# Fourteen matmuls of the identity by itself ahead of the first scores of a sparse attention and feed-forward kernel

## The chip, the core and the metric

One core of one Trainium2 chip runs the whole kernel. The metric is the device time of one execution in microseconds; of several runs the median stands.

## What is computed

The reference is a block-sparse attention followed by a gated feed-forward layer, all in float32.

```python
scores = scale * np.matmul(q, k.transpose(0, 1, 3, 2))        # q, k, v: 4 x 8 x 768 x 64
mask = np.abs(blk_i - blk_j) <= 1                             # blocks of 32 positions
mask = mask | (blk_i == 0) | (blk_j == 0) | (blk_i == 23) | (blk_j == 23)
...
        mask[qb*32:(qb+1)*32, kb*32:(kb+1)*32] = True         # three sampled blocks a query block
scores = np.where(mask, scores, -1e9)
attn = np.exp(scores - np.max(scores, axis=-1, keepdims=True))
attn = attn / (np.sum(attn, axis=-1, keepdims=True) + 1e-09)
x = np.matmul(attn, v)                                        # then 3072 tokens x 512
h = x @ w_in                                                  # 512 x 2048
g = h * (1.0 / (1.0 + np.exp(-1.702 * h)))
return g @ w_out                                              # 2048 x 512
```

## The kernel before

The attention is cut into units: 64 query positions of one batch entry, with all eight heads. Eight units make a chunk of 512 tokens, and the feed-forward layer takes one chunk at a time, while the units of the next chunk are worked on in between. The first chunk has no feed-forward work to lie beside, and its eight units are run by `first()`, in an order that is written out by hand in the string `ORDER`: each entry is a letter for a step and the number of a unit. S is `scores` (TensorE, L301: 16 matmuls of 64x32 by 256 columns for a unit, into two banks of PSUM), L the minima on VectorE (`least`, L324), E the exponentials on ScalarE (L336), T `transposes` by TensorE against the identity (L352), C the copies of these on ScalarE (L357), V `values` (L376), N the normalisation (L430), R `turn`, two more transposes (L441), H the split of their result into two parts (L448, L449), X and Y copies of keys and values that two units share, W one step of the conversion of the feed-forward weights, and G n the arrival of the n-th key buffer. The string begins "X1 G0 G1 G2 G3 S0 S1 L0 E0 L1 X2 T0 E1 S2 S3", so TensorE's queue begins with the scores of units 0 and 1, the transposes of unit 0 and the scores of units 2 and 3. The instructions keep the order in which the code issues them.

G steps put work on GpSimd's queue: a small copy that waits for the key buffer's DMAs (`landed`, L771), then the gathers of value blocks (indirect DMAs, L253), and for G3 and G4 the first fetches of the weights (L474). G4 also refills key buffer 0 from SP, behind a DMA that waits for the minima of unit 6 (L783). The weights come as 64-bit words and are turned into float32 on ScalarE and VectorE (L486 to L531), each in time for the feed-forward step that needs it.

The identity is a constant tile of 128x128 float32, `self.ident`. GpSimd writes it in `indices()`, ahead of all this, with the helper in masks.py (a memset, then an affine select). Before, its first reader is the first transpose of unit 0. The eight banks of PSUM are `self.bank[0]` to `self.bank[7]`; in the first chunk the scores use banks 0, 1, 4 and 5, the transposes 3 and 7.

The feed-forward layer multiplies in two ways. For the first eight of the 16 slices of the hidden dimension in the first chunk, `down` (L608) is a plain float32 matmul of 128x128 by 128x512. All the rest (L563 to L565, L618 to L623) are matmuls of operands that were split into a high and a low part of type float32r.

Of the kernel before, what the change touches and what calls it, by code (L numbers as in the profile page):

```python
# [18 lines left out]
P = 128  # L19
# [22 lines left out]
AHEAD = 5  # L42
NFULL = 8
FIRST = CU // 2
ORDER = """X1 G0 G1 G2 G3 S0 S1 L0 E0 L1 X2 T0 E1 S2 S3 L2 C0 T1 C1 Y1 V0 N0 L3 X3 V1 E2 T2 R0 N1 E3 H0 S4 R1 S5 C2 T3 L4 H1
V2 N2 E4 C3 L5 Y2 T4 C4 R2 H2 E5 V3 N3 S6 L6 R3 G4 S7 H3 L7 E6 T5 V4 C5 Y3 V5 N4 E7 W W R4 T6 C6 N5 W R5 H4 H5 T7 C7 W
V6 N6 W V7 W R6 W N7 H6 R7 H7 W"""
# [2 lines left out]
class Kernel:  # L50
# [4 lines left out]
    def __init__(self, ctx, tc, q, qd, kb, kT, v, vd, sb, w_in, w_out, out):  # L55
# [29 lines left out]
        self.vmid += spare[4:6]  # L85
        self.kmidof, self.vmidof = [None] * FIRST, [None] * FIRST
        self.units, self.kent, self.vent, self.items = [], [], [], []
# [23 lines left out]
        for of in (self.kent, self.vent):  # L111
            for e in of:
                e["at"] = e["n"] if e["n"] < FIRST else e["n"] % RING
        self.knext = self.vnext = FIRST
        self.most = {"scores": FIRST + 1, "values": FIRST + 1}
        self.early, self.turned = True, False
# [3 lines left out]
    def indices(self):  # L120
# [7 lines left out]
        def take(shape):  # L128
            n = 1
            for k in shape:  # L130
# [8 lines left out]

        vblk = take([NB])  # L140
        first, second = slice(1, NB - 2, 2), slice(2, NB - 1, 2)
        nc.gpsimd.iota(vblk[3 * BLK:P, first], pattern=[[2, NU]], base=0, channel_multiplier=0,
                       allow_small_or_imprecise_dtypes=True)
# [21 lines left out]
        for i in range(NR):  # L165
            for cols, rows in ((first, slice(BLK * i, BLK * (i + 1))), (second, slice(BLK * (i + 1), BLK * (i + 2)))):
                nc.vector.tensor_copy(out=vblk[rows, cols], in_=sbw[rows, cols, i])
# [28 lines left out]
    def load_k(self, e):  # L196
# [9 lines left out]
        nc.sync.dma_start(out=self.qt[r].rearrange("p b c -> p (b c)"), in_=self.q[:, b // 2, u])  # L206
        if 0 < e["n"] < FIRST:
            nc.sync.dma_start(out=kg[:, 1:9:7], in_=kb[:, q0 + 1:q0 + 3])
# [6 lines left out]
        self.sampled(e, 0, nc.sync)  # L215
        if e["n"] >= FIRST or e["n"] == 0:
            self.sampled(e, 1, nc.sync if e["n"] else nc.scalar)
# [237 lines left out]
    def weights(self):  # L455
# [40 lines left out]
        for k in range(3, AHEAD):  # L496
            fetch(k)
        yield
        first(0)
        yield  # L500
        for k, (f, i) in enumerate(todo):
# [261 lines left out]
    def first(self):  # L763

        nc, items = self.nc, self.items[:CU]
        assert self.items[CU]["unit"]["n"] == CU
        work = {}

        def landed(r):

            nc.gpsimd.tensor_copy(out=self.seen[:, 0:NPAIR].rearrange("p (a b) -> p a b", a=2), in_=self.kg[r][:, 6:12:5, 0, 0:2])  # L771

        def ahead(n):

            if n < FIRST:
                landed(n)
                self.gather(self.vent[n])
                if n + 2 < FIRST:
                    self.sampled(self.kent[n + 2], 1, nc.gpsimd)
                if n == FIRST - 1:  # L780
                    next(self.conv)
            else:
                nc.sync.dma_start(out=self.seen[:, NPAIR:2 * NPAIR], in_=items[2 * n - 2]["unit"]["nm"][:, 0])  # L783
                self.load_k(self.kent[self.knext])
                self.knext += 1
                landed(0)
                next(self.conv)
                self.loads()

        for step in ORDER.split():  # L790
            what, n = step[0], int(step[1:] or 0)
            g = items[n]
            if what == "G":
                ahead(n)
            elif what == "W":
                next(self.conv)
            elif what == "X":
                for to, of in ((0, 8), (7, 1)):
                    nc.vector.tensor_copy(out=self.kg[n][:, to], in_=self.kg[n - 1][:, of])
            elif what == "Y":  # L800
                nc.vector.tensor_copy(out=self.vmid[n][UT:P], in_=self.vmid[0][UT:P])
            elif what == "S":
                work["L", n], *work["E", n] = self.scores(g)
                work["L", n] = [work["L", n]]
            elif what == "T":
                work["C", n] = self.transposes(g)
                self.turned = n == CU - 1
            elif what == "V":
                work["N", n] = self.values(g)
            elif what == "R":  # L810
                work["H", n] = self.turn(g)
            else:
                for f in work.pop((what, n)):
                    f()
        assert not work
        x1 = self.const.tile([P, 2, NCT, CT], F32R, name="x1")
        self.x.append((x1[:, 0], x1[:, 1]))
        wout = self.const.tile([P, WRING, 2 * DM], F32R, name="wout")
        self.wout = [wout[:, i] for i in range(WRING)]
# [66 lines left out]
```

## Time and profile before

| | us |
|---|---|
| three runs: median (lowest to highest) | 772.25 (770.96 to 776.37) |
| the profiled execution: its own time | 773.84 |
| its span, from the first to the last instruction | 771.2 |
| TensorE busy in the span | 740.8 |
| VectorE, ScalarE, GpSimd busy | 408.1, 375.8, 69.8 |

The span is 2.6 us shorter than the execution's own time, since the profile begins with the first instruction of the program. All times in rows are counted from there. PE is TensorE's matmul, PEld its weight load, DVE VectorE, ACT ScalarE, POOL GpSimd, SP SyncE, which issues DMAs; a name with a q behind it (SPq) is the instruction queue of that engine. A matmul of plain float32 leaves more than one record; "x64" counts records.

### The profile page before, as it was taken

To read this page: it belongs to the slowest core of one execution; us is meant where nothing else is said; L and a number is where in the kernel's file an instruction comes from. 1 tells how busy PE (TensorE), PEld (TensorE's weight loads), DVE (VectorE), ACT (ScalarE), POOL (GpSimd) and SP (SyncE) were. 2 spreads that over 40 slices of the span, in tenths; PEclk is the share of its full clock that TensorE was granted. 3 is DMA by queue.
4 is the path that set the end of the run, shared out by engine and by line. 5 is a ranking of instruction groups with operands and counts; after the bars stand their busy time and mean duration, and the time that the engine had idled before them with its cause. 6 is when DMAs were issued, how large, how long until landed. Compare 5 with 4: busy or idle time off the path is not lost.

```text
span 771.2 us, 18922 instructions
## 1 busy us (share of the span) xinstructions
PE 740.8 (96%) x7424; PEld 563.5 (73%) x7424; DVE 408.1 (53%) x1069; ACT 375.8 (49%) x938; POOL 69.8 (9%) x112
## 2 busy tenths in 40 slices
PE   2879999999999999999999999999999999999997
PEld 1555666777787777778778777778777777888885
DVE  3588988885544434554454454454555344433332
ACT  2675666765554453544444444444554454333232
POOL 4324212120000000000000000000000000000000
PEclk9999999999999999999999999999999999999999
DMA  8979996675742546554444454345564321141211
GB/s 227 299 257 388 370 347 223 205 235 177 241 159 74 184 139 207 149 166 154 123 141 148 146 166 156 124 130 159 179 210 145 101 81 42 29 109 42 55 41 55
DMA packets 64251, 126.88 MB, mean 165 GB/s; under 512 B 7617, under 2 KB 30402, under 8 KB 63650
## 3 DMA queue, kind: packets, MB, share of 16 engines
q1 hardware_dynamic: 51970, 83.78, 36.1%
q0 software_dynamic: 11376, 41.03, 15.5%
q8 instruction: 58, 0.95, 0.5%
q10 hardware_dynamic: 816, 0.86, 0.4%
q14 instruction: 31, 0.25, 0.1%
HBM read 115.16 MB, written 10.49 MB: 163 GB/s over the span
## 4 chain that ended last, share of the span: by engine, by line
PE 92%; DMA 2%; DVE 2%; issue 1%; ACT 1%; another core or an unknown queue 1%; SPq 1%; ACTq 0%; DVEq 0%
PE bank L563 12%; PE bank L564 11%; PE bank L565 11%; PE bank L622 11%; PE bank L623 10%; PE bank L618 10%; PE bank L352 6%; PE bank L376 6%; PE bank L301 6%; PE bank L608 3%; PE bank L396 2%; PE bank L313 2%; PE bank L441 1%; DMA win<-in_moe_w_in_dram 1%
## 5 line engine op out<-in xcount | busy, mean ns | idle before, releaser
L578 DVE SCALAR_TENSOR_TENSOR g<-g,bank 128x512 f32<-128x512 f32 x83 | 57.1, 688 | 185.6 <-ACT g L571 185.6
L336 ACT ACTIVATE ex<-bank,nm 128x256 f32<-128x256 f32 (+1 forms) x176 | 84.6, 490 | 119.8 <-DVE nm L324 119.8
L622 PE MATMUL bank<-wout,ghi 128*128 128x512 f32 x352 | 141.6, 402 | 0.0
L623 PE MATMUL bank<-wout,ghi 128*128 128x512 f32 x352 | 139.5, 396 | 0.0
L571 ACT ACTIVATE g<-bank 128x512 f32<-128x512 f32 x96 | 57.3, 597 | 154.9 <-PE bank L565 153.0
L618 PE MATMUL bank<-wout,glo 128*128 128x512 f32 x352 | 99.1, 395 | 0.0
L552 DVE TENSOR_TENSOR wout<-wst,wout 128x512 fp32r<-128x512 f32 x80 | 55.4, 693 | 79.6 <-ACT wout L551 78.7
L324 DVE CUSTOM_DVE_ANT_1 bank<-bank,bias 128x256 f32<-128x256 f32 x176 | 73.8, 440 | 20.1 <-remote 8.6
L563 PE MATMUL bank<-xhi,win 128*128 128x512 f32 x192 | 80.6, 420 | 0.5 <-ACT xhi L448 0.5
L563 PE MATMUL bank<-x,win 128*128 128x512 f32 x192 | 78.8, 410 | 0.2 <-DVE g L578 0.2
L585 ACT CAST ghi<-g 128x512 fp32r<-128x512 f32 x88 | 54.7, 621 | 49.8 <-DVE g L578 49.7
L618 PEld LDWEIGHTS bank<-wout,glo 128*128 128x128 f32 x352 | 66.1, 188 | 16.0
L622 PEld LDWEIGHTS bank<-wout,ghi 128*128 128x128 f32 x352 | 66.2, 188 | 15.3
L623 PEld LDWEIGHTS bank<-wout,ghi 128*128 128x128 f32 x352 | 66.3, 188 | 14.7
L564 PE MATMUL bank<-x,win 128*128 128x512 f32 x192 | 76.1, 396 | 0.0
L564 PE MATMUL bank<-xlo,win 128*128 128x512 f32 x192 | 75.9, 395 | 0.0
L565 PE MATMUL bank<-xhi,win 128*128 128x512 f32 x192 | 75.6, 394 | 0.0
L565 PE MATMUL bank<-x,win 128*128 128x512 f32 x192 | 75.4, 393 | 0.0
L253 POOL DMA_INDIRECT vown<-in_v_dram,vidx x40 | 39.4, 986 | 380.7 <-PE bank L376 268.4
L357 ACT COPY pt<-bank 128x512 f32<-128x512 f32 (+1 forms) x112 | 56.8, 563 | 20.9 <-PE bank L352 20.9
L593 DVE TENSOR_TENSOR glo<-g,ghi 128x512 fp32r<-128x512 f32 x88 | 60.3, 685 | 1.4 <-ACT ghi L585 1.4
L301 PE MATMUL bank<-kg,qt 64*32 64x256 f32 x1280 | 47.0, 393 | 14.0 <-DMA qt<-in_q_dram 13.4
(135 smaller groups left out, 1047.3 us busy)
## 6 DMA issues: line engine op xcount, KB each, us to landing
wst<-ws SPq DMA_DIRECT2D x80, 256.0 KB
kg<-in_kb_dram SPq DMA_DIRECT2D x114, 128.0 KB
kg<-in_kb_dram SPq DMA_DIRECT2D x42, 256.0 KB
win<-in_moe_w_in_dram POOLq DMA_DIRECT2D x16, 512.0 KB
raw<-in_moe_w_out_dram POOLq DMA_DIRECT2D x16, 512.0 KB
kg<-in_kT_dram SPq DMA_DIRECT2D x4, 1536.0 KB
vown<-in_vd_dram SPq DMA_DIRECT2D x8, 768.0 KB
out_dram<-raw SPq DMA_DIRECT2D x41, 128.0 KB
```

The lines of the kernel that those rows point to most:

```text
L301: nc.tensor.matmul(sps[h][BLK * c:BLK * (c + 1), n * i:n * (i + 1)].rearrange("p (g n s) -> p g n s", g=2, s=BLK), self.qt[r][rows, bi, UT ...
L324: nc.vector.tensor_tensor_reduce(out=at, in0=at, in1=bias, scale=-SCALE, scalar=3.0e38, op0=ALU.add, op1=ALU.min, accum_out=un["nm"][:, ha ...
L336: nc.scalar.activation(out=ex, in_=sps[h][:, n * k:n * (k + 1)], func=AF.Exp, bias=un["nm"][:, half, c:c + 1], scale=-1.0, accum_out=un["r ...
L563: nc.tensor.matmul(h, wih[:, k], hi[:, k], start=(k == 0), stop=False)
L564: nc.tensor.matmul(h, wih[:, k], lo[:, k], start=False, stop=False)
L565: nc.tensor.matmul(h, wil[:, k], hi[:, k], start=False, stop=(k == NCT - 1))
L571: nc.scalar.activation(out=g, in_=self.h, func=AF.Tanh, scale=0.851)
L578: nc.vector.scalar_tensor_tensor(out=g, in0=g, scalar=1.0, in1=h, op0=ALU.add, op1=ALU.mult)
L593: self.nc.vector.tensor_tensor(out=glo, in0=g, in1=ghi.bitcast(F32), op=ALU.subtract)
L618: nc.tensor.matmul(o[n], glo[:, tk[n]], woh, start=False, stop=last)
L622: nc.tensor.matmul(o[n], ghi[:, tk[n]], woh, start=(f == 0), stop=False)
L623: nc.tensor.matmul(o[n], ghi[:, tk[n]], wol, start=False, stop=False)
```

## The change

Fourteen matmuls are issued on TensorE ahead of the loop over `ORDER`. Stationary and moving operand are the identity, the moving one read four times over, so that each has 512 columns; the result goes into bank 7, each time anew, and nobody reads it.

```diff
+WARM = 14
...
+        many = self.ident.rearrange("p (o c) -> p o c", o=1).broadcast_to([P, 4, P])
+        for _ in range(WARM):
+            nc.tensor.matmul(self.bank[7].rearrange("p (o c) -> p o c", o=4), self.ident, many, start=True, stop=True)
         for step in ORDER.split():
```

TensorE's queue at the head of the program, before: a branch into the program, then the scores of unit 0 (bank_85 and bank_86 are banks 0 and 1, kg_93 and qt_95 the first keys and queries), the first of which wait for DMAs.

```order
0 L882 UNCONDITIONAL_BRANCH [waits barrier_Pool_Activation_PE_DVE_SP_release]
1 L301 MATMUL bank_85<-kg_93,qt_95 32x256 [waits DMAHW4_49,DMAHW3_49,DMAHW6_49,DMAHW2_49,DMAHW0_49]
2 L301 MATMUL bank_86<-kg_93,qt_95 32x256
3 L301 MATMUL bank_85<-kg_93,qt_95 32x256 [waits DMAHW7_49,DMAHW5_49,DMAHW1_49]
4 L301 MATMUL bank_86<-kg_93,qt_95 32x256
```

The same place now (bank_92 is bank 7; the line numbers behind the edit are larger, L302 is what was L301).

```order
0 L886 UNCONDITIONAL_BRANCH [waits barrier_Pool_Activation_PE_DVE_SP_release]
1 L793 MATMUL bank_92<-ident 128x512 [waits Pool_49]
2 L793 MATMUL bank_92<-ident 128x512 x13
3 L302 MATMUL bank_85<-kg_93,qt_95 32x256 [waits DMAHW4_49,DMAHW3_49,DMAHW6_49,DMAHW2_49,DMAHW0_49]
4 L302 MATMUL bank_86<-kg_93,qt_95 32x256
5 L302 MATMUL bank_85<-kg_93,qt_95 32x256 [waits DMAHW7_49,DMAHW5_49,DMAHW1_49]
6 L302 MATMUL bank_86<-kg_93,qt_95 32x256
```

The scores stand behind fourteen matmuls that wait for GpSimd once, and keep their own waits for DMAs.

Further on in TensorE's queue, the transposes of unit 0 before (bank_88 and bank_92 are banks 3 and 7, ghi and glo the exponentials):

```order
33 L352 MATMUL bank_88<-ident,ghi 128x128 [waits Activation_49,Pool_49]
34 L352 MATMUL bank_88<-ident,ghi 128x128
35 L352 MATMUL bank_88<-ident,ghi 128x128 [waits Activation_49]
36 L352 MATMUL bank_88<-ident,ghi 128x128
37 L352 MATMUL bank_92<-ident,glo 128x128 [waits Activation_49]
```

And now:

```order
35 L353 MATMUL bank_88<-ident,ghi 128x128 [waits Activation_49]
36 L353 MATMUL bank_88<-ident,ghi 128x128
37 L353 MATMUL bank_88<-ident,ghi 128x128 [waits Activation_49]
38 L353 MATMUL bank_88<-ident,ghi 128x128
39 L353 MATMUL bank_92<-ident,glo 128x128 [waits Activation_49]
```

The wait for GpSimd, which wrote the identity, went from the first transpose to the first of the new matmuls; the transposes into bank 7 have no new wait. The other engines' instructions stand as they stood.

## Rows read from the trace of the kernel before

**Rows 1.** The page: busy time, and three lines of the 40 slices.
```profile
PE 740.8 (96%) x7424; PEld 563.5 (73%) x7424; DVE 408.1 (53%) x1069; ACT 375.8 (49%) x938; POOL 69.8 (9%) x112
...
PE   2879999999999999999999999999999999999997
...
PEclk9999999999999999999999999999999999999999
```
**Rows 2.** The chain of waits, 0 to 110 us: start, length, what.
```profile
10.90 6.12 another core or an unknown queue
17.02 0.41 DVE bank L324
...
18.83 0.81 PE bank L352 x4
...
26.42 1.11 issue
...
47.21 1.40 issue
...
59.08 7.03 DMA win<-in_moe_w_in_dram
...
67.82 1.20 PE bank L301 x32
...
72.02 3.43 PE bank L608 x8
```
**Rows 3.** Timeline of GpSimd: start, length, what, idle time before and releaser.
```profile
3.48 0.29 POOL masks.py:199 TENSOR_SCALAR_AFFINE_SELECT ident<-ident 128x128 f32<-128x128 f32 x1
...
54.99 0.53 POOL L771 COPY seen<-kg 128x4 f32<-128x4 f32 x1 [13.82 <-DMA kg<-in_kb_dram]
```
**Rows 4.** Timelines of TensorE's matmuls and weight loads, 13 to 30 us.
```profile
13.40 4.45 PE L301 MATMUL bank<-kg,qt 64*32 64x256 f32 x64 [13.40 <-DMA qt<-in_q_dram]
...
20.48 2.76 PE L301 MATMUL bank<-kg,qt 64*32 64x256 f32 x64
...
28.92 0.38 PE L441 MATMUL bank<-ident,x 128*128 128x128 f32 x2
...
16.87 0.33 PEld L301 LDWEIGHTS bank<-kg,qt 64*32 64x32 f32 x14 [0.55 <-issue]
...
29.23 0.70 PEld L301 LDWEIGHTS bank<-x 64*32 64x32 f32 x32 [0.17 <-DMA x<-in_kb_dram]
```
**Rows 5.** Instructions by line: 13.4 to 17.0, 17.45 to 17.5, 20.6 to 23 us; busy, mean ns.
```profile
L301 PE MATMUL bank<-kg,qt 64*32 64x256 f32 x56 | 4.2, 629 | 13.4 <-DMA qt<-in_q_dram 13.4
...
L301 PE MATMUL bank<-kg,qt 64*32 64x256 f32 x14 | 1.0, 523 | 0.0
...
L301 PE MATMUL bank<-kg,qt 64*32 64x256 f32 x64 | 2.8, 381 | 0.0
```
**Rows 6.** L608 alone: least, median and longest ns of one record.
```profile
L608 PEld LDWEIGHTS bank<-ghi,g x32: 186/190/192, 63.6 to 116.5; 128*128 128x128 f32 x32
L608 PE MATMUL bank<-ghi,g x32: 591/592/697, 63.6 to 117.0; 128*128 128x512 f32 x32
```
**Rows 7.** Windows: length, PE, PEld, DVE, ACT, POOL busy; clock, DMA share, GB/s.
```profile
44.00:52.00 8.00, 6.12 (x122) 4.82 (x120) 5.30 (x19) 6.64 (x23) 0.00 (x0) 1.00 0.92 316
52.00:54.00 2.00, 1.83 (x67) 1.60 (x67) 1.77 (x7) 1.51 (x4) 0.00 (x0) 1.00 0.30 86
...
80.00:760.00 680.00, 677.52 (x6553) 521.08 (x6546) 352.93 (x886) 328.50 (x809) 40.48 (x50) 1.00 0.48 150
```
**Rows 8.** VectorE's timeline at 17 us; SP's waits: in total, times, longest.
```profile
17.01 0.43 DVE L324 CUSTOM_DVE_ANT_1 bank<-bank,bias 128x256 f32<-128x256 f32 x1 [6.11 <-remote]
...
SPq L783 <- DVE xlo L449: 13.3, 1, 13.3
```
**Rows 9.** Window of L301 alone, TensorE: length, busy, clock, DMA share, GB/s.
```profile
13.40:15.50 2.10, 2.10 (x40) 1.00 1.07 289
```

## The prediction

> **What bounds the kernel now.** I read the page's shares first, then the chain that ended last, then the timelines of single engines around the place of the edit. TensorE is busy for 740.8 of 771.2 us, and the slices show where it is not: the first and second slice of 19.3 us each, and the end [rows 1]. From 80 to 760 us it is busy for 677.5 of 680 us, in the windows [rows 7]; nothing in front of the program can be won back or lost there, so whatever happens to the first units either reaches 68 us as a shift of everything, or is swallowed before. The question is therefore one of the first 68 us alone.
>
> In those the chain runs as follows [rows 2]: DMAs, from 10.90 on a stretch of 6.12 us that it puts down to an unknown queue, the first `least` on VectorE at 17.02 (L324), the exponentials, the first transposes on TensorE at 18.83 (L352), and then mostly TensorE, with three pieces called issue (the first of 1.11, the last of 1.40 us), in which it waits for nothing that the profile shows. At 59.08 a load of w_in takes the chain for 7.03 us, and from 67.82 on TensorE never lets go. The timeline puts names to the first stretch: the first scores start at 13.40, released by a DMA, and with the second unit's take 4.45 us for 64 records; the same 64 records at 20.48 take 2.76 us [rows 4].
>
> Why 4.45? The page's clock row shows full speed in every slice [rows 1], but one scores matmul of the first pair takes 629 ns, at 17.5 us 523 on average, and later 381 [rows 5]: of the two levels, 1.2 and 2.4 GHz, the first pair runs at the lower until about 17.4, that is for 4.0 us after TensorE's first matmul, with 13.4 us of nothing before. The row on the page can't have counted that stretch. What full speed would be worth there is 4.45 - 2.76 = 1.7 us of TensorE time, and part of the 4.45 is not clock at all: the weight loads stop for 0.55 us ahead of 16.87 [rows 4].
>
> **The change, part by part.** On TensorE's queue the 14 matmuls go ahead of the first scores; on the other engines nothing moves. They need only the identity, which GpSimd finishes at 3.48 + 0.29 = 3.77 [rows 3], so they begin at about 3.8, and the wait for GpSimd that the first transpose had is now theirs. They add no wait for what follows: bank 7 is next written by TensorE itself, in order. They cost TensorE time, though, and the question is whether they end before 13.40.
>
> What one costs is read from the matmul of the same form, L608 (128x128 f32 against 128x512 f32). Four of them in the code leave eight records, two for each, and eight take 3.43 us in the chain [rows 2], so a record takes 0.43 us at full clock and its weight load of 0.19 us lies beside the one before [rows 6]. At the half level I take twice that, 0.86, an estimate from the ratio of the two levels. Fourteen matmuls are 28 records: 28 x 0.43 = 12.0 us at full clock, 24.1 at the half. With the clock down for the first c us they end at 3.8 + 12.0 + c/2 (in c us only half the work is done). The only rise in the trace came 4.0 us after the first matmul; with c = 4.0 the end is 17.8 us. Bounds: c = 0 gives 15.8, a clock that never rises 27.9. Even the lowest is 2.4 us behind the data at 13.40, so the first scores are late in every case of this sum.
>
> What is gained against it: the scores now run at full clock. The first unit's 32 records are half of 2.76, 1.4 us, so they are done at 17.8 + 1.4 = 19.2. VectorE had them at 17.01 [rows 8]. So the first `least` comes at 17.2 + c/2 - 17.01, or 0.2 + c/2 = 2.2 us later; 0.2 at the lower end, and at the upper 27.9 + 2.1 (no more than the 2.10 us in which 40 records were begun at the half level [rows 9]) = 30.0, 13.0 us later. The second unit's scores end at 17.8 + 2.76 = 20.6, still ahead of the first transposes (1.82 us behind the first `least`, so 21.0), and hide there as before. The pause in the weight loads around 16 falls into the 14 matmuls, which need a new load only every 0.43 us; I give that nothing either way.
>
> Does the 2.2 us reach the end? The fifth unit's scores at 29.23 waited 0.17 us for a DMA, and the transposes before them end at 28.92 + 0.38 = 29.3 [rows 4]: no slack that could swallow a delay there. The refill of the first key buffer is issued from SP behind a wait of 13.3 us for VectorE's minima of the seventh unit; its DMAs find no full queue any more, the DMA share being down to 0.30 at 52 to 54 us; GpSimd sees it landed at 54.99, after 13.82 us of waiting, and only then fetches the weights whose landing at 66.11 lets ScalarE and then TensorE go on [rows 2, 3, 7, 8]. Every link waits for the one before, so I pass on all of it. From 44 to 52 us the DMA share is 0.92, and a request that comes later finds a shorter queue: up to the whole 2.2 us could go there, the lower bound being none passed.
>
> Sum: +2.2 us on the profiled execution, span 771.2 to 773.4, its own time 773.84 to 776.0. The median of the runs shown is 772.25, 1.6 below the profiled one, so the forecast for a median is 772.25 + 2.2 = 774.5.
>
> On c: the trace has one rise, 4.0 us after the start of work, so it can't tell whether c is a constant. The Trainium skill (TensorE: Matmul & The Clock Gate, Part 1) says that throttled is the resting state, that work releases it, and that the moment isn't tied to a kernel's first matmul, so that the count of slow ones differs from run to run and shouldn't be fitted. By that rule c may lie on either side of 4.0, and an edit whose count is fitted to one phase won't hold in the next; no run here shows it.
>
> **Rivals.**
> 1. The delay vanishes: the clock rises almost at once (c near 0), or the DMA queue of 44 to 52 us swallows it. For it: the DMA share of 0.92 there; against: the 0.30 that follows [rows 7], and SP's wait. Time: 772.25 to 772.5. Chance 0.18.
> 2. Slower in earnest: the identity's matmuls don't lift the clock, all 28 records run at the half level, and the first `least` comes 13.0 us late: 785.3. It decides once c is over 15 us (0.2 + c/2 above 7.7). Against it: in the trace the scores' own matmuls lifted it. Chance 0.05.
> 3. The 14 matmuls leave one record each: with c = 4.0, 4.7 records at 0.86 and 9.3 at 0.43 end at 11.8, ahead of 13.40, and the first pair gains its 1.7 us: 770.5. Against it: L608's two records per matmul. Chance 0.05. That the change doesn't lift the clock for the scores at all would be rival 2.
> 4. The 56 further records (with weight loads) in front shift where TensorE's pauses called issue fall; one more of them on the chain is 1.1 to 1.4 us [rows 2], together 775.6 to 775.9 with the 2.2. Chance 0.10.
>
> **How the numbers follow.** The forecast, +1 to +4 us, has 0.60, the rivals 0.38, the rest 0.02. The range goes from rival 3 with a little of the scatter of the runs (770) past rival 4 and a c of up to 12 us (778.5). A measurement of this kernel tells about 1% (7.7 us) from no change. Only rival 2, and scatter, is beyond it: slower 0.07. Faster by over 1% has no case, 0.03 for what I don't see; within 1% is 0.90.
>
> **What would show it.** In the changed profile: 28 records of 128x512 f32 from about 3.8 us, the first four or five about twice as long as the rest; the last ending near 17.8; 64 scores records behind it at about 381 ns; the first `least` near 19.2; the w_in load and the first full-speed stretch (67.82 before) later by about the same 2.2 us. Scores that begin at 13.4 would make rival 3 right, slow records throughout rival 2, a `least` that is late with 67.82 unmoved rival 1.

## The result, and the profile after

| us | before | after |
|---|---|---|
| median of six runs on the same chip (lowest to highest) | 773.71 (770.96 to 776.88) | 780.43 (780.05 to 782.11) |
| profiled execution: span | 771.2 | 778.9 |
| forecast for the median | | 774.5 (770.0 to 778.5) |

After takes 1.0081 times as long as before, with a 95% interval of 1.0054 to 1.0108. That is 6.7 us more, where 2.2 were forecast: the sign was right, the size was a third of what came, and the time lies above the range.

The page of after shows the work itself hardly changed. TensorE has 14.8 us more of busy time than in [rows 1]; 13.9 of it are the 28 new records, in the first slice:

```profile
span 778.9 us, 18977 instructions
...
PE 755.6 (97%) x7452; PEld 568.2 (73%) x7452; DVE 408.1 (52%) x1069; ACT 375.7 (48%) x938; POOL 69.4 (9%) x112
...
PE   7886999999999999999999999999999999999997
```

The stretch from 80 to 760 us is as full as it was (677.52 of 680 us in [rows 7]); the clock stands below full speed in two short windows. Windows of after (length, PE, PEld, DVE, ACT, POOL busy; clock, DMA share, GB/s):

```profile
24.30:27.60 3.30, 3.30 (x58) 1.73 (x66) 1.46 (x8) 2.64 (x10) 0.18 (x1) 0.50 1.01 345
75.50:78.80 3.30, 3.30 (x23) 2.11 (x7) 3.27 (x8) 1.32 (x2) 0.00 (x0) 0.50 1.04 395
80.00:760.00 680.00, 678.09 (x6575) 519.72 (x6574) 356.12 (x896) 332.69 (x822) 40.71 (x51) 1.00 0.49 153
```

So everything happened in front. The timeline of TensorE's matmuls after, from the start (start, length, what, idle time before and its end):

```profile
3.82 13.94 PE L793 MATMUL bank<-ident 128*128 128x512 f32 x28 [3.82 <-POOL ident masks.py:199]
...
17.70 2.38 PE L302 MATMUL bank<-kg,qt 64*32 64x256 f32 x49
20.25 1.49 PE L302 MATMUL bank<-kg,qt 64*32 64x256 f32 x15 [0.17 <-issue]
22.84 0.89 PE L353 MATMUL bank<-ident,ghi 128*128 128x128 f32 x4 [1.09 <-ACT ghi L337]
23.75 1.13 PE L353 MATMUL bank<-ident,glo 128*128 128x128 f32 x4
24.81 3.33 PE L302 MATMUL bank<-kg,qt 64*32 64x256 f32 x64
```

The new matmuls begin at 3.82 and end at 17.76, as forecast (3.8 and 17.8). The scores behind them are short, as forecast: the instructions by line give 381 ns from 17.7 to 19 us (629 in [rows 5]). But the clock that was won is lost again: after TensorE's idle time ahead of 22.84 the window above shows it at half speed, and the scores of units 2 and 3 at 24.81 take 3.33 us in place of 2.76 [rows 4]. By line (busy us, mean ns), 17.7 to 19 and 24.8 to 27.2 us:

```profile
L302 PE MATMUL bank<-kg,qt 64*32 64x256 f32 x45 | 1.6, 381 | 0.0
...
L302 PE MATMUL bank<-kg,qt 64*32 64x256 f32 x48 | 2.8, 631 | 0.0
```

The scores of the first pair don't take the 1.96 us that 64 of them take undisturbed (this row comes again in E8), but 4.04 us, from 17.70 to 21.74. TensorE's weight loads show three holes of 0.57 to 0.61 us, each put down to nothing (after, timeline of PEld; the 0.76 us of the first row are no hole: before the first scores' weights, behind the new matmuls, the same 0.76 us stand in E8, where no gather is running):

```profile
17.69 1.21 PEld L302 LDWEIGHTS bank<-kg,qt 64*32 64x32 f32 x47 [0.76 <-issue]
19.51 0.15 PEld L302 LDWEIGHTS bank<-kg,qt 64*32 64x32 f32 x3 [0.61 <-issue]
20.27 0.13 PEld L302 LDWEIGHTS bank<-kg,qt 64*32 64x32 f32 x2 [0.60 <-issue]
20.97 0.29 PEld L302 LDWEIGHTS bank<-kg,qt 64*32 64x32 f32 x12 [0.57 <-issue]
```

VectorE's first `least` then starts at 21.11 (17.01 in [rows 8]), though unit 0's scores had ended at 18.79:

```profile
21.11 0.43 DVE L325 CUSTOM_DVE_ANT_1 bank<-bank,bias 128x256 f32<-128x256 f32 x1 [10.49 <-remote]
```

What else went on is on GpSimd: its two pairs of gathers. The timeline of GpSimd after:

```profile
13.04 1.02 POOL L254 DMA_INDIRECT vown<-in_v_dram,vidx  x1 [0.58 <-issue]
14.37 0.97 POOL L254 DMA_INDIRECT vown<-in_v_dram,vidx  x1 [0.30 <-issue]
...
18.19 0.99 POOL L254 DMA_INDIRECT vown<-in_v_dram,vidx  x1 [0.17 <-issue]
19.48 0.97 POOL L254 DMA_INDIRECT vown<-in_v_dram,vidx  x1 [0.30 <-issue]
```

and of before, where the first pair stands in the same place behind G0:

```profile
14.13 1.02 POOL L253 DMA_INDIRECT vown<-in_v_dram,vidx  x1 [0.58 <-issue]
15.46 0.97 POOL L253 DMA_INDIRECT vown<-in_v_dram,vidx  x1 [0.30 <-issue]
```

Before, the second gather ends at 16.43 and the first `least` starts 0.58 later, though its scores were done at 15.47. After, the second gather of G1 ends at 20.45 and the first `least` starts 0.66 later. In both, VectorE starts behind a pair of gathers and not behind the scores; the change pushed the scores from G0's pair into G1's. It isn't VectorE that hesitates: the semaphore that TensorE raises for unit 0's scores is recorded in the trace at 16.98 before and at 21.08 after, 0.03 us ahead of VectorE's start. TensorE's signal is late, or its matmuls, whose ends the profile models, ended later than it says.

The chain of waits after, 0 to 80 us (start, length, what), answers to [rows 2]:

```profile
10.62 10.51 another core or an unknown queue
21.12 0.41 DVE bank L325
...
38.31 0.60 issue
...
44.12 1.17 issue
...
56.71 3.20 DMA kg<-in_kb_dram
60.02 0.60 POOL seen L772
...
64.21 8.83 DMA win<-in_moe_w_in_dram
...
74.74 1.54 PE bank L302 x32
```

The delay grows on its way. It is 4.1 us at the first `least`. (Before's profile is itself late there: GpSimd sees the first keys at 13.37 in it and at 12.28 in after. In E2, E6 and E11 below, where it sees them at 12.35, the first `least` starts at 16.02 to 16.06, so with like data the change costs 5.1 us at this place.) The pause of 1.17 us stands in unit 6's scores, and the seventh unit's minima, for which SP's refill waits, come 4.1 us late. GpSimd sees the refill at 60.02 in place of 54.99 [rows 3], 5.0 us late. The fetch of w_in goes out 5.1 us late (64.21 for 59.08) and takes 8.83 us in place of 7.03. Its end is 6.9 us late, feed-forward slice 2 starts 7.3 us late (76.20 for 68.94), and the span is 7.7 us longer.

Slices 0 and 1, whose weights are fetched ahead of the refill, start only 2.8 us late (59.57 for 56.76, 62.70 for 59.88). The rest is added ahead of slice 2. There ScalarE's queue holds the first step on the weights of the late fetch in front of slice 1's gate and of the copy for which TensorE waits. ScalarE and then TensorE, before:

```profile
66.13 0.69 ACT L486 ACTIVATE a<-win 128x512 f32<-128x512 f32 x1 [1.32 <-DMA win<-in_moe_w_in_dram]
...
67.82 1.20 PE L301 MATMUL bank<-kg,qt 64*32 64x256 f32 x32 [0.56 <-ACT wst L576]
```

and after:

```profile
73.07 0.66 ACT L487 ACTIVATE a<-win 128x512 f32<-128x512 f32 x1 [4.69 <-DMA win<-in_moe_w_in_dram]
...
74.74 1.54 PE L302 MATMUL bank<-kg,qt 64*32 64x256 f32 x32 [3.91 <-ACT wst L577]
```

ScalarE waits 3.4 us longer for these weights, and TensorE 3.4 us longer for ScalarE.

### The profile page after: what moved, and what is told of

Read it like the earlier page. It is cut to its first block, busy times and chain, and to the rows that moved or that the text cites. A ratio compares the mean times of both kernels' runs of the same rounds, so it can differ in the third digit from the quotient of the medians.

```text
span 778.9 us, 18977 instructions
## 1 busy us (share of the span) xinstructions
PE 755.6 (97%) x7452; PEld 568.2 (73%) x7452; DVE 408.1 (52%) x1069; ACT 375.7 (48%) x938; POOL 69.4 (9%) x112
## 4 chain that ended last, share of the span: by engine, by line
PE 90%; DMA 3%; another core or an unknown queue 2%; SPq 1%; issue 1%; ACT 1%; DVE 1%; POOL 0%; DVEq 0%; ACTq 0%; POOLq 0%
PE bank L564 12%; PE bank L565 11%; PE bank L566 11%; PE bank L623 10%; PE bank L624 10%; PE bank L619 10%; PE bank L353 6%; PE bank L302 5%; PE bank L377 5%; PE bank L609 3%; PE bank L397 2%; PE bank L314 2%; PE bank L442 1%; DMA win<-in_moe_w_in_dram 1%
## 5 line engine op out<-in xcount | busy, mean ns | idle before, releaser
L623 PE MATMUL bank<-wout,ghi 128*128 128x512 f32 x352 | 141.6, 402 | 0.0
L564 PE MATMUL bank<-xhi,win 128*128 128x512 f32 x192 | 81.1, 422 | 0.5 <-ACT xhi L449 0.5
L564 PE MATMUL bank<-x,win 128*128 128x512 f32 x192 | 78.7, 410 | 0.2 <-DVE g L579 0.2
L623 PEld LDWEIGHTS bank<-wout,ghi 128*128 128x128 f32 x352 | 66.2, 188 | 15.4
L565 PE MATMUL bank<-xlo,win 128*128 128x512 f32 x192 | 76.3, 397 | 0.0
L565 PE MATMUL bank<-x,win 128*128 128x512 f32 x192 | 76.0, 396 | 0.0
L302 PE MATMUL bank<-kg,qt 64*32 64x256 f32 x1280 | 47.1, 394 | 4.3 <-ACT wst L577 3.9
```

What stands on the lines that cost most here:

```text
L302: nc.tensor.matmul(sps[h][BLK * c:BLK * (c + 1), n * i:n * (i + 1)].rearrange("p (g n s) -> p g n s", g=2, s=BLK), self.qt[r][rows, bi, UT ...
L564: nc.tensor.matmul(h, wih[:, k], hi[:, k], start=(k == 0), stop=False)
L565: nc.tensor.matmul(h, wih[:, k], lo[:, k], start=False, stop=False)
L623: nc.tensor.matmul(o[n], ghi[:, tk[n]], woh, start=(f == 0), stop=False)
```

## The experiments

The theory that came out of this comparison has two halves. One: VectorE's first `least` can't start while GpSimd works on a pair of gathers, so a late start of the scores costs a step and not its own length. Two: the lateness grows behind that, at GpSimd's wait for the refill of the key buffer. The rivals: the clock (the two falls in after are what costs); the records (the 28 new ones shift TensorE's pauses called issue); and the extra work of TensorE itself, with no place. The expectations below were written before each run and name the theories in their own words. Their ranges lean on before's 772 to 774 us; each ratio compares with runs of before on the same chip, whose medians lay from 773.30 to 775.27 us, and is the better measure.

One table holds what the profiles of all runs show, so that the text need not repeat it: the start of the first scores, the end of unit 0's scores, the first `least`, the seventh unit's minima, GpSimd seeing the refill, the start of slice 2 of the feed-forward layer, and the span.

| | scores start | unit 0 done | first least | minima 7 | refill seen | slice 2 | span |
|---|---|---|---|---|---|---|---|
| before | 13.40 | 15.47 | 17.01 | 42.02 | 54.99 | 68.94 | 771.2 |
| after | 17.70 | 18.79 | 21.11 | 46.16 | 60.02 | 76.20 | 778.9 |
| E1, 8 matmuls | 13.04 | 14.14 | 15.88 | 41.26 | 55.74 | 72.54 | 775.7 |
| E2, 14 tiny | 12.39 | 14.47 | 16.02 | 40.13 | 54.62 | 68.43 | 771.4 |
| E3, held | 21.16 | 23.11 | 23.20 | 44.97 | 59.52 | 75.50 | 771.0 |
| E4, before, G0 plain | 12.04 | 14.12 | 14.17 | 41.82 | 54.95 | 70.72 | 772.3 |
| E5, held, same tiles | 17.26 | 19.22 | 20.94 | 46.10 | 60.83 | 77.25 | 779.4 |
| E6, before + 4 bytes | 12.39 | 14.47 | 16.06 | 39.66 | 52.82 | 68.65 | 764.7 |
| E7, after + 4 bytes | 18.85 | 19.94 | 20.89 | 44.04 | 57.90 | 74.82 | 771.2 |
| E8, 20 matmuls | 23.14 | 24.24 | 24.33 | 47.72 | 61.73 | 78.50 | 781.1 |
| E9, after, G1 plain | 18.27 | 19.37 | 19.46 | 46.55 | 60.84 | 76.66 | 779.8 |
| E10, E1 + G0 plain | 12.46 | 13.67 | 13.73 | 45.13 | 59.88 | 75.69 | 777.8 |
| E11, before + 64 bytes | 12.38 | 14.46 | 16.03 | 41.77 | 56.87 | 72.37 | 774.2 |
| E12, E6, late gathers | 12.24 | 14.32 | 14.37 | 42.09 | 57.69 | 74.09 | 769.4 |
| E13, before, no wait | 11.95 | 14.03 | 15.65 | 40.49 | | 67.20 | 770.0 |
| E14, after, no wait | 17.75 | 18.84 | 20.94 | 46.26 | | 71.15 | 773.0 |
| E15, E6, no wait | 12.30 | 14.38 | 15.94 | 40.34 | | 66.62 | 762.0 |

**E1: eight matmuls instead of fourteen.** They end before the data arrive, so it keeps the clock and drops the lateness.

```diff
-WARM = 14
+WARM = 8
```

> Eight matmuls of the identity in place of fourteen. By the changed kernel's rows (3.82 us start, four records at 0.86 us, the rest at 0.43) the sixteen records end near 12.4 us, ahead of the data at 12.3 to 13.4. Theory A (the loss comes from scores that begin late, at 17.70 in place of 13.40): the scores start at about 13 us at full clock, and the time is that of the kernel before or up to 2 us less, 771 to 774. Theory B (56 more records in front move TensorE's instruction pauses, and these cost the time): half of the loss or more stays, 776 to 780. Theory C (a clock that falls again later costs the time): it falls again behind the early matmuls as in the changed kernel, 775 to 780.

Measured: 776.65 us, ratio 1.0008 [0.9978, 1.0039]. In microseconds this is above theory A's range and inside those of B and C; by the ratio, before on that chip being at 774.82, nothing was lost that can be measured. Part of theory C did happen: after the fast scores the clock falls again at 28.7, 56.0 and 69.6 us. The matmuls end at 13.11 and the scores are fast, 3.47 us for the pair, with unit 0 done at 14.14. Yet the first `least` comes at 15.88, 0.6 us behind the second gather (15.27). Timelines of TensorE and of VectorE in E1:

```profile
3.83 9.28 PE L793 MATMUL bank<-ident 128*128 128x512 f32 x16 [3.83 <-POOL ident masks.py:199]
...
13.04 3.47 PE L302 MATMUL bank<-kg,qt 64*32 64x256 f32 x64
...
15.88 0.43 DVE L325 CUSTOM_DVE_ANT_1 bank<-bank,bias 128x256 f32<-128x256 f32 x1 [5.25 <-remote]
```

What a full clock wins on the first scores is given to the wait behind the gathers, and the end doesn't move: this prologue isn't bound by TensorE's speed.

**E2: fourteen matmuls of one column.** The instructions stay, their time goes.

```diff
-            nc.tensor.matmul(self.bank[7].rearrange("p (o c) -> p o c", o=4), self.ident, many, start=True, stop=True)
+            nc.tensor.matmul(self.bank[7][:, 0:1], self.ident, self.ident[:, 0:1], start=True, stop=True)
```

> Fourteen matmuls with the same records (28 and their weight loads) but one column each, so that they are over by about 7 us. Theory A: the scores start with their data at about 13.4 us, at the half clock as before; 772 to 775. Theory B (the number of records in front moves the instruction pauses): the loss stays, 777 to 781.

Measured: 775.27 us, ratio 1.0016 [0.9984, 1.0049]. Its first `least`, with scores at the half clock and data as early as in E1, starts at 16.02, only 0.14 us behind E1's. More records in front cost nothing that can be measured; the rival of the records falls, as far as 14 instructions go.

**E3: no matmuls, but the scores held back.** Fourteen copies of ScalarE from the first key buffer into bank 7, and one matmul of one column that reads their result, stand ahead of the scores.

```diff
+        held = self.const.tile([P, 1], F32, name="held")
+        for _ in range(14):
+            nc.scalar.copy(out=self.bank[7], in_=self.kg[0].rearrange("p n b c -> p (n b c)")[:, 1024:1536])
+        nc.scalar.copy(out=held, in_=self.bank[7][:, 0:1])
+        nc.tensor.matmul(self.bank[7][:, 0:1], self.ident, held, start=True, stop=True)
```

> No matmuls of the identity but one of a single column that waits for fourteen idle copies on ScalarE (10 to 17.4 us), so that the scores start at about 17.7 us with a clock that is still down. Theory A: lateness alone makes the loss; 780 to 784, the higher end if the half clock adds its 1.7 us. Theories B and C: most of the loss is gone, 773 to 777.

Measured: 773.49 us, ratio 0.9982 [0.9949, 1.0015]; theory A's 780 to 784 is missed. Scores that start 7.8 us late, and slice 2 that starts 6.6 us late, at no cost: against the theory, if it were all. But the table shows slice 2 as late as in after and the span as short as before's, so some 6 us were won behind it, in a part of the program that wasn't touched. From slice 16 of the feed-forward layer to the end it takes 580.9 us; before takes 586.8, after 587.0. What differs is the new tile `held` of 4 bytes a partition. E5 to E7 and E11 take the two apart.

**E4: before, with the first pair of gathers as plain loads.** The first key group's value blocks are then not the sampled ones.

```diff
+            if e["n"] in (0,):
+                self.nc.gpsimd.dma_start(out=self.vblocks[e["at"]][j], in_=self.v[e["b"] // 2][P * j:P * (j + 1)])
+                continue
```

> The kernel before, with the two gathers of value blocks behind G0 (indirect DMAs of GpSimd at 14.1 and 15.5 us) replaced by plain DMAs of as many rows from GpSimd: the first key group's value blocks are then not the sampled ones. Theory S (the pauses in TensorE's weight loads at 15.6 to 16.9 and the late start of the first minima, 17.01 against scores that end at 15.47, come from the gathers): the weight loads run on, the first two units' scores end by 17.0 and the first minima start by 15.7. Theory S' (they come from the program's place, or from the half clock): both stand as they were, first minima at 17.0.

Measured: 773.95 us in a single execution (before on the chip: 774.82). Without gathers in front, the first `least` starts 0.05 us after unit 0's scores. VectorE's timeline in E4:

```profile
14.17 0.43 DVE L327 CUSTOM_DVE_ANT_1 bank<-bank,bias 128x256 f32<-128x256 f32 x1 [3.69 <-PE bank L304]
```

The releaser reads "PE" here, where it read "remote". The first half of the theory holds: the lag behind the scores is 0.05 us in place of 1.5. The first `least` is 2.8 us earlier than in before's profile, but 1.4 of them come from data that landed earlier (scores start at 12.04 for 13.40). All of it is gone by the seventh unit's minima (41.82 for 42.02).

**E5: held back again, with no new tile.** E3 with ten copies, and a column of an existing tile in place of `held`.

```diff
+        for _ in range(10):
+            nc.scalar.copy(out=self.bank[7], in_=self.kg[0].rearrange("p n b c -> p (n b c)")[:, 1024:1536])
+        nc.scalar.copy(out=self.seen[:, 7:8], in_=self.bank[7][:, 0:1])
+        nc.tensor.matmul(self.bank[7][:, 0:1], self.ident, self.seen[:, 7:8], start=True, stop=True)
```

> As e3_hold, but without its new tile of 4 bytes a partition (an unused column of an existing tile takes its place) and with ten copies, so that the scores start near 18 us at the half clock. e3 started late (21.2 us), lost 6.6 us by the third feed-forward slice (75.5 against 68.9 us) and won 5.3 us back afterwards, when its feed-forward matmuls came at 229 ns where the other kernels' come at 232 to 237. Theory A (lateness makes the loss; e3 won it back by an unrelated gain that its new tile brought): no such gain here, 777 to 782, and the third slice begins at 72 to 76 us. Theory A' (lateness is made up later by itself): 772 to 776.

Measured: 779.68 us, ratio 1.0058 [1.0027, 1.0089]. TensorE does nothing new, its clock is down for the first scores (4.76 us for the pair), and it loses 5.7 us all the same. Slice 2 starts at 77.25, a little later than expected. TensorE in E5:

```profile
17.26 4.76 PE L301 MATMUL bank<-kg,qt 64*32 64x256 f32 x64
```

The loss is that of the late start; neither the 28 records nor their time on TensorE are needed for it.

**E6 and E7: before and after, each with an unused tile of 4 bytes a partition** among the constants.

```diff
+        self.const.tile([P, 1], F32, name="held")
         for step in ORDER.split():
```

> The kernel before with one more tile of 4 bytes a partition that nothing uses, allocated at the place where e3 had its own. If the gain of e3 came from where the later tiles lie: the feed-forward slices 16 to 88 pass in 5 us less than before's 545.0, and the time is 767 to 770. If not: 545.0 and 772 to 776.

> The changed kernel with the same unused tile. If the two effects add: the loss at the head stays (the third feed-forward slice at 74 to 77 us) and the slices behind run 5 us faster, 774 to 776. If e3's gain came from elsewhere: 779 to 782.

Measured: E6 768.41 us, 0.9921 [0.9889, 0.9952]; E7 773.79 us, 1.0015 [0.9988, 1.0042]. From slice 16 to the end both take what E3 took, 580.8 and 580.7 us (before's 545.0 us of the expectations run from slice 16 to slice 90). Against each other they stand 5.4 us apart: the change costs about the same on the faster footing. So E3's null was a loss of some 6 us and a gain of 6 us from another place.

**E8: twenty matmuls.** The scores now start at 23.14, behind both pairs of gathers.

```diff
-WARM = 14
+WARM = 20
```

> Twenty matmuls in place of fourteen: twelve more records of 0.43 us, so that the scores start 5.2 us later, at 22.9. Theory A (what is late at the scores is late at the end, at about one for one): 784 to 787. If the loss is a step that comes with any late start (a missed place in a queue): 780 to 782.

Measured: 781.70 us, ratio 1.0086 [1.0058, 1.0115]. TensorE and VectorE in E8:

```profile
3.83 19.39 PE L793 MATMUL bank<-ident 128*128 128x512 f32 x40 [3.83 <-POOL ident masks.py:199]
23.14 1.96 PE L302 MATMUL bank<-kg,qt 64*32 64x256 f32 x64
...
24.33 0.43 DVE L325 CUSTOM_DVE_ANT_1 bank<-bank,bias 128x256 f32<-128x256 f32 x1 [13.69 <-PE bank L302]
```

With no gather beside them, the 64 records take 1.96 us and the first `least` follows unit 0's scores at 0.09 us. The scores start 5.4 us later than in after; the first `least` comes only 3.2 later, and the seventh unit's minima 1.6. The time isn't a straight line in the number of matmuls: nothing at 8, 6.7 us at 14, 7.7 at 20. It lies in the range of the step and not in that of one for one.

**E9: after, with the second pair of gathers as plain loads** (E4's edit for group 1; the second key group's value blocks are then not the sampled ones).

> The changed kernel with the two gathers behind G1 (indirect DMAs at 18.2 and 19.5 us) replaced by plain DMAs of as many rows from GpSimd; the second key group's value blocks are then not the sampled ones. Theory S (TensorE's signal to VectorE is held up until 0.6 us behind the second gather of a pair): the first minima start within 0.3 us of the end of the first scores, at 18.9 to 19.1 in place of 21.1, and of the loss of 6 us about 2 us go: 776 to 779. Theory S' (the held signal belongs to the place in the program or to the matmuls in front): first minima at 21 us, 779 to 782.

Measured: 779.98 us, ratio 1.0067 [1.0037, 1.0096]. At the place itself it does what the theory says: 1.96 us for the pair, the first `least` 0.09 us behind unit 0's scores and 1.65 us earlier than in after. At the end nothing of that is left. TensorE and VectorE in E9:

```profile
18.27 1.96 PE L305 MATMUL bank<-kg,qt 64*32 64x256 f32 x64
...
30.43 0.27 PE L380 MATMUL bank<-vown,wst 128*32 128x64 f32 x2 [2.74 <-issue]
...
38.73 0.61 PE L356 MATMUL bank<-ident,ghi 128*128 128x128 f32 x3 [2.89 <-issue]
...
19.46 0.43 DVE L328 CUSTOM_DVE_ANT_1 bank<-bank,bias 128x256 f32<-128x256 f32 x1 [8.53 <-PE bank L305]
```

Two pauses of 2.74 and 2.89 us for which the profile names no releaser ate more than was won. The first, from 27.69 to 30.43, lies on the pair of gathers behind G2 (27.45 to 29.73) and ends 0.7 us behind it, as the first `least` did behind G1's pair in after. GpSimd in E9:

```profile
27.45 0.99 POOL L257 DMA_INDIRECT win<-in_v_dram,vidx  x1 [0.52 <-issue]
28.75 0.98 POOL L257 DMA_INDIRECT win<-in_v_dram,vidx  x1 [0.31 <-issue]
```

So what was won in front of one pair seems to have been lost at the next; this is read from the times, and no run tests it. The second pause has no gather beside it. That VectorE waits behind gathers is shown, but not that the 1.9 us by which the first `least` came later than forecast (4.1 for 2.2) are part of the 6.7 at the end.

**E10: E1 with E4's edit**, fast scores and nothing in VectorE's way.

> Eight matmuls of the identity, and the gathers behind G0 replaced by plain DMAs as in e4 (the first key group's value blocks are not the sampled ones). Theory S: what full clock saves on the first scores (1.0 us: e1's took 1.10 us, before's 2.07) was hidden behind the gathers and now shows: scores from 13.0 to 14.1, first minima at 14.2. Theory S': the first minima stay at 15.9.

Measured: 779.47 us in a single execution (before: 773.3). The first `least` starts at 13.73, the earliest of all, and the fifth unit's scores then wait for their keys. TensorE in E10:

```profile
31.30 2.06 PE L305 MATMUL bank<-x 64*32 64x256 f32 x32 [4.35 <-DMA x<-in_kb_dram]
```

In this execution an early start of the first units runs into the next load, and there is nothing to win in front of it. Why it ended 6 us later than before isn't shown. These keys landed late (GpSimd sees them at 31.40; in before at 29.32, in E1 at 25.09), and its mean clock, 0.989, is the lowest of the profiled executions together with E1's; a single execution can't tell chance from the edit.

**E11: E6 with 64 bytes instead of 4** (`[P, 16]`).

> The kernel before with an unused tile of 64 bytes a partition where e6 had 4 bytes. If the gain of e6 hangs on how the later tiles lie to a small unit (64 bytes or less), the slices 16 to 88 pass in before's 545.0 us again. If any shift does it, in 539.5.

Measured: 776.45 us in a single execution (before: 773.3), 586.4 us from slice 16 to the end. A shift of the later tiles by 64 bytes brings nothing; by 4 bytes it brings 6 us. The matmuls by line, 200 to 720 us, in before, then in E6, then in E11 (busy us, mean ns):

```profile
L623 PE MATMUL bank<-wout,ghi 128*128 128x512 f32 x280 | 111.0, 396 | 0.0
L564 PE MATMUL bank<-x,win 128*128 128x512 f32 x155 | 61.4, 396 | 0.0
```

```profile
L623 PE MATMUL bank<-wout,ghi 128*128 128x512 f32 x284 | 111.3, 392 | 0.0
L564 PE MATMUL bank<-x,win 128*128 128x512 f32 x159 | 62.3, 392 | 0.0
```

```profile
L623 PE MATMUL bank<-wout,ghi 128*128 128x512 f32 x283 | 111.9, 395 | 0.0
```

In the same 520 us E6 gets through more of them, and in these two lines each is 4 ns shorter; in the other lines of the split matmuls it is 0 to 4 ns. In E11 some lines are shorter and some longer (L564 394 ns for 396, L565 395 for 393), and nothing is left in the sum.

**E12: E6, with the gathers of G0 issued together with those of G1**, to let the first `least` go.

```diff
-                self.gather(self.vent[n])
+                if n == 1:
+                    self.gather(self.vent[0])
+                if n > 0:
+                    self.gather(self.vent[n])
```

> The kernel of e6 with the gathers of the first key group behind those of G1's arrival, at 18 us, in place of 13.1 to 15.4. Theory S: the first minima start 0.1 us behind the first scores, at 14.6 in place of 16.1, and the second pair's scores or minima, which now meet four gathers, lose some of it again: 766 to 769 (e6: 768.4). If the four gathers cost more than they free: 769 to 772.

Measured: 770.17 us, ratio 0.9944 [0.9908, 0.9979], against E6's 0.9921: no gain. The first `least` starts at 14.37, 0.05 us behind its scores. The third unit's then comes behind all four gathers, the last of which ends at 21.85: VectorE stands idle for 4.80 us ahead of it. VectorE in E12:

```profile
23.27 0.43 DVE L324 CUSTOM_DVE_ANT_1 bank<-bank,bias 128x256 f32<-128x256 f32 x1 [4.80 <-remote]
```

The wait moves with the gathers, from unit 0 to unit 2.

**E13, E14 and E15: before, after and E6 without GpSimd's wait for the refill.** The small copy of G4 that waits for the refilled key buffer goes; the fetches of weights behind it no longer wait.

```diff
                 self.knext += 1
-                landed(0)
                 next(self.conv)
```

> The kernel before without GpSimd's small copy that waits for the refilled key buffer (G4), so that the weight fetches behind it go out near 45 us in place of 55. Theory R (the wait for the refill carries what is late at the head to the weights and so to the end): the third feed-forward slice begins earlier than before's 68.9 us, 65 to 68, and the time is 769 to 772. Theory R' (the fetches then fight with the refill for the DMA queues): 773 to 777.

> The changed kernel without the same copy. Theory R: the loss against e13 shrinks to the lateness of the scores themselves or less, 2 to 4 us: 772 to 775. Theory R': it stays 5 to 7 us above e13.

> e13 with the unused tile of 4 bytes of e6. If the two add: 5.5 us below e13, 763 to 767. Otherwise near e6's 768.4.

Measured, all against 775.27: E13 771.92 us, 0.9959 [0.9936, 0.9982]; E14 773.90 us, 0.9995 [0.997, 1.0021]; E15 764.72 us, 0.9868 [0.982, 0.9915]. The fetch of w_in that after issues at 64.21 goes out at 45.25, 19 us earlier. GpSimd in E14:

```profile
45.25 0.58 POOL L475 DMA_DIRECT2D win<-in_moe_w_in_dram  x1
```

The seventh unit's minima are 5.8 us later in E14 than in E13, more than the 4.1 between after and before, but between the medians only 2.0 us are left of 6.7. The two ratios, E14's and E13's, differ by 0.0036, with intervals that overlap a little, where after's and before's differ by 0.0081: the wait that was taken away is the road by which more than half of the loss came to the end. Slices 0, 1 and 2 all start 3.94 to 3.95 us later in E14 than in E13 (71.15 for 67.20 at slice 2), so nothing is added ahead of slice 2 any more; the span is 3.0 us longer. E15 is faster than both kernels.

## Why the prediction was right about the sign and wrong about the size

**Right.** The 28 records, the start at 3.8, four slow ones of 0.85 us at the head, the end at 17.8, the scores at 381 ns behind them and a first `least` that is late: all there. That even the lowest bound ended behind the data at 13.40 gave the sign, and E1 shows the other side of it, where eight matmuls end in time and cost nothing.

**The step that failed first: "the first `least` comes at 17.2 + c/2 - 17.01, or 0.2 + c/2 = 2.2 us later".** It measures the new end of the scores against the old start of the `least`, as if VectorE had waited for the scores before. It hadn't: unit 0's scores were done at 15.47, 1.5 us ahead of 17.01, with a releaser called "remote" in [rows 8] and a stretch of an "unknown queue" in [rows 2] that should have made me ask. What it waited for was GpSimd's pair of gathers. The scores were forecast done at 19.2 and were done at 18.79; the `least` came at 21.11. In six kernels without a running pair (E3, E4, E8, E9, E10, E12) VectorE follows at 0.05 to 0.09 us, in all the others at 0.95 to 2.3. The pause in the weight loads, to which I gave "nothing either way" because it would fall into the new matmuls, belongs to the gathers: it didn't stay at 16 us but came again with G1's pair, three times.

**The step that failed next: "Every link waits for the one before, so I pass on all of it".** One for one was too little on this road: 4.1 us at the first `least` became 5.0 at the refill, 6.9 at the landing of w_in and 7.7 at the end of the span. (From 4.1 to 5.0 it may not have grown at all: with like data the first is 5.1.) On the road of the units themselves it was too much, since slices 0 and 1 start only 2.8 us late. The links were the right ones: taking one out (E13, E14) leaves 2.0 of the 6.7. What isn't one for one are the lengths between: the fetch of w_in took 1.8 us longer, and 13.95 us from the refill to slice 2 before are 16.18 after. Over the 14 profiles that have that wait, the start of slice 16 goes closely with the moment GpSimd sees the refill (correlation 0.96) and only loosely with the first `least` (0.65). E4, E9 and E10 say the same: up to 3 us won or lost at the first `least` need not reach the end.

**The rivals.** The delay that vanishes and the clock that never rises didn't happen, nor did one record for each matmul. The fourth, pauses that shift, is there, but not as a loss: after has 0.60 and 1.17 us of them on its chain from 17 to 50 us, the 1.17 in unit 6's scores, and before has 1.11, 1.12 and 1.40 at other places. E2 shows that 14 more instructions alone cost nothing that can be measured.

**The clock.** Before, it rose 4.06 us after TensorE's first matmul; after, 3.37; in E1 4.4. The Trainium skill (TensorE: Matmul & The Clock Gate, Part 1) says that the moment isn't tied to a kernel's first matmul and that a count shouldn't be fitted to it; these three rises agree. The Trainium skill says in the same part that an idle engine goes back to the throttled state. The fall at 75.46 in after, behind 3.91 us in which TensorE stood idle, agrees; the one at 24.26 came with 1.09 us of idle time and TensorE at work on either side of it. At the head the clock decides nothing: E5 with a low one there loses 5.7 us, E1 with a high one gains nothing. Later it has a small part. Over 210 runs of all kernels, each compared with those of its own kernel on its chip, a mean granted clock that is lower by 0.001 goes with 0.53 us more (0.42 to 0.64). After's six runs have 0.9935 in the mean, the 92 runs of before that list a clock 0.9956; by that, an estimate, about 1.1 of the 6.7 us go with the clock. It seems to follow from the late weights: TensorE stands idle until 74.74 in after, the clock is at half from 75.46 to 78.87, and slices 2 and 3 take 16.50 us for before's 15.30. A fall between 62 and 81 us comes in all ten profiles whose slice 2 starts later than 72 us, and in E6; in E13 to E15, where the weights come early, there is none.

**Open.** Why TensorE's signals and its weight loads stand still during a pair of gathers: the profile shows that they do, not what they share. Nor do they at every pair: in before's second, from 19.27 to 21.55, the signals for unit 0's transposes are recorded at 19.65 and 20.56, 0.01 us behind their ends. So "can't start" is too strong as a rule; it held for the first scores in every kernel where a pair was running when they ended. Whether the 1.9 us of this are part of the 6.7: E9 was to show it, and its own pauses, one of them on the next pair, covered it. And why the fetch of w_in takes 7.0 us in one profile and 8.8 in another.

## What to carry to other kernels

Before work is put in front of an engine to warm it up, ask what the first reader of its result really waits for; if the answer is "remote" or "an unknown queue", look at what the other engines do at that moment, since a faster engine gains nothing there and a later one may fall into the next such wait. A late start of the first units is passed on by whatever refills a buffer behind them, and that wait is worth taking out before anything is tuned ahead of it. And when an experiment adds a tile, compare a stretch that the edit can't have touched, or run the same tile alone in the old kernel.

## What the runs showed of the hardware that was not expected

- While GpSimd issues a pair of gathers, TensorE's signal for finished scores, and with it VectorE's start, can come as late as 0.6 us after the second one's end (16.43 to 17.01, 20.45 to 21.11, in E1 15.27 to 15.88), and TensorE's weight loads pause for about 0.6 us at a time (0.55 in before, 0.57 to 0.61 in after). Plain loads by GpSimd in the same place do nothing of the kind (0.05 us in E4).
- An unused tile of 4 bytes a partition, which shifts the tiles allocated behind it, makes part of the split float32r matmuls shorter (L564 and L623 392 ns in place of 396), and the program from slice 16 on 6 us shorter (580.8 for 586.8), in five kernels out of five; one of 64 bytes does nothing (586.4). Which tile it is, wasn't tried.
- Pauses of TensorE's queue with no releaser are from 0.6 to 2.9 us long, and come at other places in each kernel; two of them undid a gain of 1.65 us in E9, where the first fell on a pair of gathers.
